# Score matmuls on partition halves, and a new order of scores and attention x V

## The chip, the cores and the metric

The kernel runs on one core of a Trainium2 chip. The metric is the device time of one execution in microseconds (us); the median of several runs counts. The engines are TensorE (PE; its weight loads are listed apart as PEld), VectorE (DVE), ScalarE (ACT), GpSimd (POOL) and SyncE (SP), which here issues every DMA transfer.

## The reference

Sigmoid attention for 2 batches of 12 heads, 448 tokens and head size 64, then an RMS norm, a gated MLP and a SiLU MLP over 896 tokens of 768 features. The MLP weights are float64.

```python
scores = scale * np.matmul(q, k.transpose(0, 1, 3, 2)) - np.log(S)
attn = 1.0 / (1.0 + np.exp(-scores))
attn_out = np.matmul(attn, v)                       # per batch and head
x = attn_out.transpose(0, 2, 1, 3).reshape(B * S, H * D)
xn = x / np.sqrt(np.mean(x * x, -1, keepdims=True) + 1e-6) * rms_g
g = xn @ w_gate
x = (g * sigmoid(g) * (xn @ w_val)) @ w_out         # 768 -> 1536 -> 768
h = x @ w_in                                        # 768 -> 2048
out = (h * sigmoid(h)) @ w_out2                     # 2048 -> 768
```

## The kernel before, in words

Everything is kept feature-major: features on the 128 partitions, tokens along the free dimension. A float32 operand is split into two float32r parts, a high part (a rounded copy) and a low part (the value minus the copy), and a product is made of several matmuls of such parts. Attention x V is a plain float32 matmul, which shows in the trace as two TensorE records per matmul.

**Attention** goes over 12 pairs of heads, a pair being two heads of one batch. For pair i, `load_pair` (lines 157 to 162) brings keys and queries from arrays in which the host has stored every head twice, once on each half of the partitions: a tile is [128, 2 heads, 448]. `prep` (lines 168 to 179) makes the parts. `ks` holds the high part of the keys on partitions 0 to 63 and the low part on 64 to 127; `qs` holds the high part of the queries on both halves, and beside it the low part on both halves. So one matmul over 128 rows computes (high + low keys) x high queries, a second one the same with low queries: two per head in `scores` (lines 181 to 194), for one chunk of 112 keys and all 448 queries. A pair has four chunks. A tile of keys or queries is 448 KB; for pair 0 each head's half, 224 KB, is loaded by itself. One ScalarE instruction then reads both heads' scores from PSUM and writes the sigmoids (line 193). `attend` multiplies a chunk with V, the two heads into the two halves of the output partitions, accumulating over the four chunks (line 202). `collect` copies two pairs' outputs from PSUM; `square` and `add_squares` gather the squares for the RMS norm.

The order is written by hand (`manual_schedule`): every engine runs its instructions in the order in which the program lists them. In pair i's turn the program lists the split of pair i+1, the loads of pair i+2, and then per chunk c: scores of (i, c), attention x V of (i-1, c), and one step of a generator. For pairs 1 to 7 that generator converts the first four weight slabs (float64 words to float32r parts, ScalarE and VectorE); from pair 8 on it is the first batch's norm: square sums by matmul (line 242), reciprocal root on VectorE (lines 249 to 259), its spread over the partitions by a matmul (line 269), and the scaling.

All PSUM is one pool of four tiles of two banks, [128, 2, 512] floats. A chunk's scores take one tile, a head to each bank; an attention x V result takes one for two pairs.

**The MLPs** follow from line 360 on, every product through `product` (line 106), with weight slabs loaded and converted ahead. The first two gate units' first batch is computed ahead of them while the second batch is normed.

Of the kernel before, what the change touches and what calls it, by code (L numbers as in the profile page):

```python
# [8 lines left out]
F32 = mybir.dt.float32  # L9
# [11 lines left out]
P = 128  # L21
# [10 lines left out]
def tile_attention_two_mlps(  # L32
    ctx: ExitStack,
    tc: tile.TileContext,
    qd: bass.AP,
    kd: bass.AP,
    vd: bass.AP,
# [4 lines left out]
):  # L42
    """sigmoid attention -> RMS norm -> gated MLP -> SiLU MLP, feature-major throughout.

    Every float32 product is hi*hi + lo*hi + hi*lo of float32r halves (12 + 12 bits), except
    attention x V, which is a plain float32 matmul. The float64 weights are narrowed to float32 on chip:
    P = the high word read as float32; P * 2^-112 moves the 11-bit exponent to float32's bias, the
    shift by 3 lines it up, and the sign and the low word's top 3 bits are put in.
    """
    nc = tc.nc  # L50
# [10 lines left out]

# [1 line left out]
    nslab = wd.shape[0]  # L63
# [7 lines left out]
    def convert(s):  # L71
        """Yields between steps, so that no engine's queue waits behind another's step."""
        words = raw_t.pop(s).rearrange("p (n two) -> p n two", two=2)
        low, high = words[:, :, 0], words[:, :, 1]
        f = wtmp.tile([P, SLAB], F32, tag="f", name=f"f{s}")
        fu = f.bitcast(U32)
        nc.scalar.activation(f, high.bitcast(F32), AF.Copy, scale=2.0**-112)  # L77
        yield
        nc.vector.tensor_scalar(fu, fu, 3, None, ALU.logical_shift_left)  # L79
        nc.vector.scalar_tensor_tensor(fu, high, 0x80000000, fu, ALU.bitwise_and, ALU.bitwise_or)  # L80
        nc.vector.scalar_tensor_tensor(fu, low, 29, fu, ALU.logical_shift_right, ALU.bitwise_or)  # L81
        yield
        yield
        t = wsp.tile([P, 2, SLAB], F32R, tag="w", name=f"w{s}")
        nc.scalar.activation(t[:, 0, :], f, AF.Copy)  # L85
        yield
        nc.vector.tensor_tensor(t[:, 1, :], f, t[:, 0, :].bitcast(F32), ALU.subtract)  # L87
        slab_t[s] = t
# [5 lines left out]
    def split(dst, src):  # L94
        """dst[:, 0] + dst[:, 1] = src, in float32r halves."""
        nc.scalar.activation(dst[:, 0], src, AF.Copy)  # L96
        nc.vector.tensor_tensor(dst[:, 1], src, dst[:, 0].bitcast(F32), ALU.subtract)  # L97

    def product(ps, tiles, acts, bs, last=True):
        """ps[:, b, :S] += W^T x for the weight tiles and activations given, over b in bs."""  # L100
        n = len(tiles)
        for i, (w, a) in enumerate(zip(tiles, acts)):
            whi, wlo = wtile(w)
            for lhs, j in ((whi, 0), (whi, 1), (wlo, 0)):
                for b in bs:
                    nc.tensor.matmul(  # L106
                        ps[:, b, :S],
                        lhs,
                        a[:, j, b * S : (b + 1) * S],
                        start=(i == 0 and j == 0 and lhs is whi),  # L110
                        stop=(i == n - 1 and lhs is wlo),
                    )
            if last and w % 6 == 5:
                del slab_t[w // 6]
                ahead(w // 6 + 1 + AHEAD)
# [15 lines left out]
    def ahead(s):  # L131
        """Slabs before s converted, and the loads two slabs on."""
        fetch(s + 2)
        while sched[0] < min(s, nslab):
            for _ in convert(sched[0]):
                pass
            sched[0] += 1
# [7 lines left out]

# [1 line left out]
    ctx.enter_context(tc.manual_schedule())  # L147
    with ExitStack() as actx:
        ap = actx.enter_context(tc.tile_pool(name="ap", bufs=2))
        at = actx.enter_context(tc.tile_pool(name="at", bufs=6))  # L150
        npool = actx.enter_context(tc.tile_pool(name="npool", bufs=1))

        pairs = [(b, hp) for b in range(B) for hp in range(NP)]
        qr, kr, vr, qs, ks, att, av, xraw, acc = {}, {}, {}, {}, {}, {}, {}, {}, {}

        def load_pair(i):
            b, hp = pairs[i]
            kr[i] = ap.tile([P, 2, S], F32, tag="kr", name=f"kr{i}")
            qr[i] = ap.tile([P, 2, S], F32, tag="qr", name=f"qr{i}")
            for hs in (slice(0, 1), slice(1, 2)) if i == 0 else (slice(0, 2),):  # L160
                nc.sync.dma_start(kr[i][:, hs], kd[b, hp, :, hs])  # L161
                nc.sync.dma_start(qr[i][:, hs], qd[b, hp, :, hs])  # L162

# [4 lines left out]
        def prep(i):  # L168
            k, q = kr.pop(i), qr.pop(i)
            ks[i] = kst = ap.tile([P, 2, S], F32R, tag="ks", name=f"ks{i}")  # L170
            qs[i] = qst = ap.tile([P, 2, 2, S], F32R, tag="qs", name=f"qs{i}")
            for hs in (slice(0, 1), slice(1, 2)) if i == 0 else (slice(0, 2),):
                nc.vector.tensor_copy(kst[:, hs], k[:, hs])
                if i:
                    nc.vector.tensor_copy(qst[:, 0, hs], q[:, hs])
                else:
                    nc.scalar.activation(qst[:, 0, hs], q[:, hs], AF.Copy)  # L177
                nc.vector.tensor_tensor(kst[D:, hs], k[D:, hs], kst[D:, hs].bitcast(F32), ALU.subtract)  # L178
                nc.vector.tensor_tensor(qst[:, 1, hs], q[:, hs], qst[:, 0, hs].bitcast(F32), ALU.subtract)  # L179

        def scores(i, c):
            ps = ps_tile(f"sc{i}_{c}")
            for h in range(2):
                for j in range(2):
                    nc.tensor.matmul(  # L185
                        ps[:CP, h, :S],
                        ks[i][:, h, c * CP : (c + 1) * CP],
                        qs[i][:, j, h, :],
                        start=(j == 0),
                        stop=(j == 1),  # L190
                    )
            a = at.tile([CP, 2, S], F32, tag="a", name=f"a{i}_{c}")
            nc.scalar.activation(a, ps[:CP, :, :S], AF.Sigmoid, bias=logs[:CP], scale=D**-0.5)  # L193
            att[i, c] = a
# [15 lines left out]
        def collect(i):  # L210
            """Two pairs' outputs from PSUM, and their squares."""
            b, hp = pairs[i]
            if hp % 2 == 0:
                return
            ps = av.pop(i // 2)
            t = npool.tile([P, 2, S], F32, tag=f"xr{b}_{hp // 2}", name=f"xr{b}_{hp // 2}")
            nc.vector.tensor_copy(t, ps[:, :, :S])
            xraw[b, hp // 2] = t
            fresh.append((b, hp))
# [19 lines left out]
        def square_sums(b, ps):  # L239
            """ps[t, c] = the sum of squares of token c * 112 + t."""  # L240
            for c in range(NC):
# [4 lines left out]
        def rsqrt(b, ps):  # L246
            """diag[t, c, u] = eye[t, u] / rms of token c * 112 + t; Newton steps from the exponent's half."""
            ms, y, t = (npool.tile([CP, NC], F32, tag=n, name=f"{n}{b}") for n in ("ms", "y", "t"))
# [18 lines left out]
        def spread(ps, diag):  # L267
            """ps[:, t] = 1 / rms of token t, on every partition."""
            nc.tensor.matmul(ps, ones[:CP], diag.rearrange("p c u -> p (c u)"), start=True, stop=True)  # L269

        def normed(b, r):
            """Yields between steps, like convert."""
            xn, xs = {}, {}
# [40 lines left out]
        for i in range(n):  # L314
# [5 lines left out]
            if i == 0:  # L320
                fetch(1)
            for c in range(NC):
                scores(i, c)
                if c == 1:
                    square()
                if c == 3:
                    add_squares()
                if i:
                    attend(i - 1, c)
                if 0 < i <= NP + 1 and c:  # L330
                    next(weights, None)
                if i > NP + 1:
                    next(normal, None)
            if i:
# [6 lines left out]

        # the first two gate units' first batch, while the second batch is normed
        for _ in itertools.chain(weights, normal):
# [15 lines left out]

# [1 line left out]
    hp_ = ctx.enter_context(tc.tile_pool(name="hp", bufs=1))  # L361
# [44 lines left out]
def _slabs(w, nk):  # L406
    """[K, M] float64 as 64-bit words: 128 x 128 tiles, output chunk by output chunk, six to a slab."""
    import numpy as np
# [42 lines left out]
```

## Time and profile before

| | us |
|---|---|
| median of 3 runs | 605.83 (604.96 to 1182.08) |
| span of the profiled execution | 604.1 |
| busy in it: TensorE, its weight loads | 592.8, 503.4 |
| busy in it: VectorE, ScalarE | 354.1, 230.1 |

The page names the profiled execution's span, from its first to its last instruction; the median run is 1.7 us above it (605.83 - 604.1), and no further time of that execution is listed. The mean granted TensorE clock is 0.999. Busy times of engines overlap. TensorE's two rows are the matmuls and the weight loads that run beside them.

### The profile page before, as it was taken

The page shows a single profiled execution, that of the slowest core. Times are in us where ns is not written, and L with a number is a line of the kernel's source. Part 1 is how long each engine was busy: PE and PEld are TensorE (multiplying, and loading weights), DVE is VectorE, ACT ScalarE, POOL GpSimd, SP SyncE. Part 2 cuts the span into 40 slices and gives each one's busy share as a digit, 9 for nine tenths or more (in the row PEclk, how much of TensorE's full clock was granted, in tenths as well). Part 3 has the DMA queues.
Part 4 walks back from the last instruction along what each step waited for, and adds up shares of the span by engine and source line. Part 5 has one row for each costly group of instructions (what it writes and reads, how often), then busy time and mean ns, then how long its engine had stood idle before and what let it go on. Part 6 is the DMA issues. An engine that isn't in the chain of part 4 may idle for free.

```text
span 604.1 us, 6969 instructions
## 1 busy us (share of the span) xinstructions
PE 592.8 (98%) x2852; PEld 503.4 (83%) x2852; DVE 354.1 (59%) x444; ACT 230.1 (38%) x271; POOL 0.2 (0%) x4
## 2 busy tenths in 40 slices
PE   4999999999999999999999999999999999999997
PEld 3444445999999999999999999999999999999996
DVE  4788793767766666666555554666666555545500
ACT  4676574344433333333333223444444432222100
POOL 0000000000000000000000000000000000000000
PEclk9999999999999999999999999999999999999999
DMA  8655540024333333232433333233332343433000
GB/s 248 225 204 206 204 144 0 1 105 150 132 137 105 105 105 105 104 105 104 129 123 115 105 105 105 105 105 105 104 105 104 106 143 120 134 135 136 30 31 30
DMA packets 16383, 70.49 MB, mean 117 GB/s; under 512 B 2080, under 2 KB 2848, under 8 KB 16352
## 3 DMA queue, kind: packets, MB, share of 16 engines
q1 hardware_dynamic: 16352, 70.05, 34.0%
q8 instruction: 22, 0.36, 0.3%
q14 instruction: 9, 0.07, 0.0%
HBM read 67.29 MB, written 2.75 MB: 116 GB/s over the span
## 4 chain that ended last, share of the span: by engine, by line
PE 97%; DMA 1%; DVE 1%; SPq 0%; issue 0%
PE e L106 19%; PE i L106 19%; PE g L106 15%; PE v L106 15%; PE o L106 14%; PE sc L185 7%; PE av L202 7%; DMA qr<-in_q 1%; SPq L161 0%; DVE ks L178 0%; DVE qs L179 0%; PE r L269 0%; PE ms L242 0%; SPq L162 0%; PE v L269 0%; PE v L242 0%
## 5 line engine op out<-in xcount | busy, mean ns | idle before, releaser
L85 ACT ACTIVATE w<-f 128x768 fp32r<-128x768 f32 x68 | 57.5, 846 | 277.8 <-PE i L106 62.7
L87 DVE TENSOR_TENSOR w<-f,w 128x768 fp32r<-128x768 f32 x68 | 65.2, 958 | 150.4 <-ACT w L85 150.4
L106 PE MATMUL e<-g,w 128*128 128x448 f32 x576 | 116.9, 365 | 0.0
L106 PE MATMUL i<-y,w 128*128 128x448 f32 x576 | 116.9, 365 | 0.0
L106 PEld LDWEIGHTS i<-y,w 128*128 128x128 f32 x576 | 108.2, 188 | 8.5
L106 PEld LDWEIGHTS e<-g,w 128*128 128x128 f32 x576 | 108.2, 188 | 8.5
L106 PE MATMUL g<-x,w 128*128 128x448 f32 x432 | 90.3, 366 | 0.0
L106 PE MATMUL v<-x,w 128*128 128x448 f32 x432 | 89.9, 365 | 0.0
L106 PE MATMUL o<-h,w 128*128 128x448 f32 x432 | 87.7, 365 | 0.0
L106 PEld LDWEIGHTS g<-x,w 128*128 128x128 f32 x432 | 81.1, 188 | 7.5 <-issue 0.9
L106 PEld LDWEIGHTS o<-h,w 128*128 128x128 f32 x432 | 81.2, 188 | 6.4
L106 PEld LDWEIGHTS v<-x,w 128*128 128x128 f32 x432 | 81.1, 188 | 6.4
L185 PEld LDWEIGHTS sc<-qs,ks 128*112 128x112 f32 x192 | 31.5, 182 | 42.0 <-issue 24.9
L80 DVE SCALAR_TENSOR_TENSOR f<-raw,f 128x768 uint32<-128x768 uint32 x68 | 65.2, 958 | 2.3
L81 DVE SCALAR_TENSOR_TENSOR f<-raw,f 128x768 uint32<-128x768 uint32 x68 | 65.2, 958 | 2.4
L185 PE MATMUL sc<-qs,ks 128*112 128x448 f32 x192 | 53.9, 404 | 7.7 <-ACT qs L177 7.2
L77 ACT ACTIVATE f<-raw 128x768 f32<-128x768 f32 x68 | 60.8, 894 | 1.1 <-DMA raw<-in_w 1.1
L193 ACT ACTIVATE a<-sc,logs 112x896 f32<-112x896 f32 x48 | 48.2, 1007 | 27.6 <-PE sc L185 27.0
L202 PE MATMUL av<-a,vr 112*64 112x448 f32 x192 | 45.8, 562 | 0.0
L79 DVE TENSOR_SCALAR f<-f 128x768 uint32<-128x768 uint32 x68 | 37.6, 553 | 4.5 <-ACT f L77 4.5
L401 DVE COPY out<-e 128x896 f32<-128x896 f32 (+1 forms) x7 | 6.7, 957 | 32.3 <-PE e L106 32.3
L97 DVE TENSOR_TENSOR g<-sg,g 128x896 fp32r<-128x896 f32 x16 | 17.5, 1093 | 13.3 <-ACT g L96 13.3
(49 smaller groups left out, 198.1 us busy)
## 6 DMA issues: line engine op xcount, KB each, us to landing
raw<-in_w SPq DMA_DIRECT2D x68, 768.0 KB, 4.2
kr<-in_k SPq DMA_DIRECT2D x11, 448.0 KB, 5.0
qr<-in_q SPq DMA_DIRECT2D x11, 448.0 KB, 5.6
vr<-in_v SPq DMA_DIRECT2D x12, 224.0 KB, 2.8
out_t<-out SPq DMA_DIRECT2D x5, 448.0 KB, 2.5
kr<-in_k SPq DMA_DIRECT2D x2, 224.0 KB, 3.3
qr<-in_q SPq DMA_DIRECT2D x2, 224.0 KB, 4.2
out_t<-out SPq DMA_DIRECT2D x2, 224.0 KB, 1.9
```

Source lines behind the costliest of these rows:

```text
L77: nc.scalar.activation(f, high.bitcast(F32), AF.Copy, scale=2.0**-112)
L79: nc.vector.tensor_scalar(fu, fu, 3, None, ALU.logical_shift_left)
L80: nc.vector.scalar_tensor_tensor(fu, high, 0x80000000, fu, ALU.bitwise_and, ALU.bitwise_or)
L81: nc.vector.scalar_tensor_tensor(fu, low, 29, fu, ALU.logical_shift_right, ALU.bitwise_or)
L85: nc.scalar.activation(t[:, 0, :], f, AF.Copy)
L87: nc.vector.tensor_tensor(t[:, 1, :], f, t[:, 0, :].bitcast(F32), ALU.subtract)
L97: nc.vector.tensor_tensor(dst[:, 1], src, dst[:, 0].bitcast(F32), ALU.subtract)
L106: nc.tensor.matmul(ps[:, b, :S], lhs, a[:, j, b * S : (b + 1) * S], start=(i == 0 and j == 0 and lhs is whi), stop=(i == n - 1 and lhs is ...
L185: nc.tensor.matmul(ps[:CP, h, :S], ks[i][:, h, c * CP : (c + 1) * CP], qs[i][:, j, h, :], start=(j == 0), stop=(j == 1),)
L193: nc.scalar.activation(a, ps[:CP, :, :S], AF.Sigmoid, bias=logs[:CP], scale=D**-0.5)
L202: nc.tensor.matmul(ps[h * D : (h + 1) * D, hp % 2, :S], vr[i][:, c, h, :], a[:, h, :], start=(c == 0), stop=(c == NC - 1),)
L401: nc.vector.tensor_copy(o[:, sl], ps[:, sl, :S])
```

## The change

Keys and queries are no longer stored twice. The host lays a pair's two heads on the two halves of the partitions, keys and queries side by side in one array, and one tile `kq` (three buffers) holds both. `prep` makes the high part of the whole tile and the low part of the whole tile. `scores` runs three matmuls per head on 64 rows each, high x high, high keys x low queries, low keys x high queries, the two heads in turns; the product of the two low parts is not computed any more. In the loop over chunks, two chunks' scores are followed by attention x V of two chunks, and the generators' steps stand behind them, three and four per pair as before. The sigmoid tiles have eight buffers instead of six.

```diff
-        at = actx.enter_context(tc.tile_pool(name="at", bufs=6))
+        at = actx.enter_context(tc.tile_pool(name="at", bufs=8))
...
-            kr[i] = ap.tile([P, 2, S], F32, tag="kr", name=f"kr{i}")
-            qr[i] = ap.tile([P, 2, S], F32, tag="qr", name=f"qr{i}")
-            for hs in (slice(0, 1), slice(1, 2)) if i == 0 else (slice(0, 2),):
-                nc.sync.dma_start(kr[i][:, hs], kd[b, hp, :, hs])
-                nc.sync.dma_start(qr[i][:, hs], qd[b, hp, :, hs])
+            kq[i] = ap.tile([P, 2, S], F32, tag="kq", name=f"kq{i}", bufs=3)
+            if i:
+                nc.sync.dma_start(kq[i], qkd[b, hp])
+            else:
+                for j in range(2):
+                    nc.sync.dma_start(kq[i][:, j], qkd[b, hp, :, j])
...
-            ks[i] = kst = ap.tile([P, 2, S], F32R, tag="ks", name=f"ks{i}")
-            qs[i] = qst = ap.tile([P, 2, 2, S], F32R, tag="qs", name=f"qs{i}")
-            for hs in (slice(0, 1), slice(1, 2)) if i == 0 else (slice(0, 2),):
-                nc.vector.tensor_copy(kst[:, hs], k[:, hs])
-                if i:
-                    nc.vector.tensor_copy(qst[:, 0, hs], q[:, hs])
-                else:
-                    nc.scalar.activation(qst[:, 0, hs], q[:, hs], AF.Copy)
-                nc.vector.tensor_tensor(kst[D:, hs], k[D:, hs], kst[D:, hs].bitcast(F32), ALU.subtract)
-                nc.vector.tensor_tensor(qst[:, 1, hs], q[:, hs], qst[:, 0, hs].bitcast(F32), ALU.subtract)
+            raw = kq.pop(i)
+            ks[i] = kst = ap.tile([P, 2, 2, S], F32R, tag="ks", name=f"ks{i}")
+            if i:
+                nc.vector.tensor_copy(kst[:, 0], raw)
+                nc.vector.tensor_tensor(kst[:, 1], raw, kst[:, 0].bitcast(F32), ALU.subtract)
+            else:
+                nc.vector.tensor_copy(kst[:, 0, 0], raw[:, 0])
+                nc.scalar.activation(kst[:, 0, 1], raw[:, 1], AF.Copy)
+                for j in (1, 0):
+                    nc.vector.tensor_tensor(
+                        kst[:, 1, j], raw[:, j], kst[:, 0, j].bitcast(F32), ALU.subtract
+                    )
...
-            for h in range(2):
-                for j in range(2):
+            for step, (jk, jq) in enumerate(((0, 0), (0, 1), (1, 0))):
+                for h in range(2):
+                    rows = slice(h * D, (h + 1) * D)
                     nc.tensor.matmul(
                         ps[:CP, h, :S],
-                        ks[i][:, h, c * CP : (c + 1) * CP],
-                        qs[i][:, j, h, :],
-                        start=(j == 0),
-                        stop=(j == 1),
+                        ks[i][rows, jk, 0, c * CP : (c + 1) * CP],
+                        ks[i][rows, jq, 1, :],
+                        start=(step == 0),
+                        stop=(step == 2),
                     )
...
-            for c in range(NC):
+            for c in range(0, NC, 2):
                 scores(i, c)
-                if c == 1:
+                scores(i, c + 1)
+                if c == 0:
                     square()
-                if c == 3:
+                else:
                     add_squares()
                 if i:
                     attend(i - 1, c)
-                if 0 < i <= NP + 1 and c:
-                    next(weights, None)
-                if i > NP + 1:
-                    next(normal, None)
+                    attend(i - 1, c + 1)
+                for _ in range(1 if c == 0 else 2):
+                    if 0 < i <= NP + 1:
+                        next(weights, None)
+                for _ in range(2):
+                    if i > NP + 1:
+                        next(normal, None)
...
     def headwise(a):
-        t = a.transpose(0, 1, 3, 2).reshape(B, NP, 2, D, S).transpose(0, 1, 3, 2, 4)
-        return np.ascontiguousarray(np.concatenate([t, t], axis=2))
+        return a.transpose(0, 1, 3, 2).reshape(B, NP, P, S)
...
-        "q": headwise(q),
-        "k": headwise(k),
+        "kq": np.ascontiguousarray(np.stack([headwise(k), headwise(q)], axis=3)),
```

## Rows read from the trace of the kernel before

**Rows 1.** The page's chain that ended last: share of the span by line.
```profile
PE e L106 19%; PE i L106 19%; PE g L106 15%; PE v L106 15%; PE o L106 14%; PE sc L185 7%; PE av L202 7%; DMA qr<-in_q 1%; SPq L161 0%; DVE ks L178 0%; DVE qs L179 0%; PE r L269 0%; PE ms L242 0%; SPq L162 0%; PE v L269 0%; PE v L242 0%
```

**Rows 2.** Stretches: length; busy us (count) PE, PEld, DVE, ACT, POOL; clock; DMA share; GB/s.
```profile
0.00:14.44 14.44, 6.77 (x17) 4.38 (x17) 6.97 (x13) 6.17 (x8) 0.20 (x4) 1.00 0.88 246
14.44:67.49 53.05, 53.05 (x224) 22.70 (x224) 42.25 (x52) 36.75 (x40) 0.00 (x0) 1.00 0.61 221
```

**Rows 3.** Timeline of TensorE, two chunks: start us, us, line, out<-in, count.
```profile
40.86 1.06 PE L185 MATMUL sc<-qs,ks 128*112 128x448 f32 x4
...
41.85 0.97 PE L202 MATMUL av<-a,vr 112*64 112x448 f32 x4
...
42.76 1.08 PE L185 MATMUL sc<-qs,ks 128*112 128x448 f32 x4
...
44.67 0.46 PE L185 MATMUL sc<-qs,ks 128*112 128x448 f32 x1
```

**Rows 4.** Timeline inside the first of those chunks, from narrow windows.
```profile
41.15 0.57 PE L185 MATMUL sc<-qs,ks 128*112 128x448 f32 x2
...
41.16 0.17 PEld L185 LDWEIGHTS sc<-qs,ks 128*112 128x112 f32 x1
...
41.56 0.37 PE L185 MATMUL sc<-qs,ks 128*112 128x448 f32 x1
...
42.28 0.55 PE L202 MATMUL av<-a,vr 112*64 112x448 f32 x2
```

**Rows 5.** Chain in order of time, one MLP product: start us, us, what.
```profile
148.15 7.30 PE g L106 x36
```

**Rows 6.** Timeline after the last scores: five chunks of attention x V.
```profile
98.56 3.98 PE L202 MATMUL av<-a,vr 112*64 112x448 f32 x20
...
98.99 0.14 PEld L202 LDWEIGHTS av<-a,vr 112*64 112x64 f32 x2 [0.23 <-issue]
...
101.62 0.14 PEld L202 LDWEIGHTS av<-a,vr 112*64 112x64 f32 x2 [0.23 <-issue]
...
102.47 0.88 PE L106 MATMUL g<-x,w 128*128 128x448 f32 x3
```

**Rows 7.** Groups by line and shape, 0 to 150 us: busy us, mean ns, idle before.
```profile
L193 ACT ACTIVATE a<-sc,logs 112x896 f32<-112x896 f32 x48 | 48.2, 1007 | 27.6 <-PE sc L185 27.0
...
L179 DVE TENSOR_TENSOR qs<-qr,qs 128x896 fp32r<-128x896 f32 x11 | 12.0, 1092 | 0.3
...
L77 ACT ACTIVATE f<-raw 128x768 f32<-128x768 f32 x10 | 8.9, 891 | 1.1 <-DMA raw<-in_w 1.1
...
L175 DVE CAST qs<-qr 128x896 fp32r<-128x896 f32 x11 | 6.8, 621 | 1.7 <-DMA qr<-in_q 1.7
...
L225 ACT ACTIVATE sq<-xr 128x896 f32<-128x896 f32 x6 | 5.7, 944 | 4.0 <-DVE xr L217 4.0
```

**Rows 8.** Timeline of the start, 0 to 20 us.
```profile
4.51 0.63 DVE L179 TENSOR_TENSOR qs<-qr,qs 128x448 fp32r<-128x448 f32 x1
...
4.56 1.35 PE L185 MATMUL sc<-qs,ks 128*112 128x448 f32 x2 [4.56 <-ACT qs L177]
...
7.91 0.58 ACT L177 ACTIVATE qs<-qr 128x448 fp32r<-128x448 f32 x1 [3.42 <-DMA qr<-in_q]
...
8.53 5.42 PE L185 MATMUL sc<-qs,ks 128*112 128x448 f32 x15 [2.62 <-ACT qs L177]
...
9.75 0.63 DVE L173 CAST ks<-kr 128x896 fp32r<-128x896 f32 x1 [0.61 <-DMA kr<-in_k]
...
13.30 1.09 DVE L179 TENSOR_TENSOR qs<-qr,qs 128x896 fp32r<-128x896 f32 x1
...
14.44 0.86 PE L185 MATMUL sc<-qs,ks 128*112 128x448 f32 x3 [0.49 <-DVE qs L179]
```

**Rows 9.** Timeline of the first batch's norm on VectorE: first step, diagonal.
```profile
70.94 0.15 DVE L249 TENSOR_SCALAR ms<-ms 112x4 f32<-112x4 f32 x1
...
73.31 0.62 DVE L259 TENSOR_TENSOR diag<-eye,y 112x448 f32<-112x448 f32 x1
```

More of the change, by code (lines that the diff above doesn't have):

```diff
@@ L34, in tile_attention_two_mlps @@
     tc: tile.TileContext,
-    qd: bass.AP,
-    kd: bass.AP,
+    qkd: bass.AP,
     vd: bass.AP,
@@ L149, in tile_attention_two_mlps @@
         ap = actx.enter_context(tc.tile_pool(name="ap", bufs=2))
-        at = actx.enter_context(tc.tile_pool(name="at", bufs=6))
+        at = actx.enter_context(tc.tile_pool(name="at", bufs=8))
         npool = actx.enter_context(tc.tile_pool(name="npool", bufs=1))
         pairs = [(b, hp) for b in range(B) for hp in range(NP)]
-        qr, kr, vr, qs, ks, att, av, xraw, acc = {}, {}, {}, {}, {}, {}, {}, {}, {}
+        kq, vr, ks, att, av, xraw, acc = {}, {}, {}, {}, {}, {}, {}
         def load_pair(i):
             b, hp = pairs[i]
-            kr[i] = ap.tile([P, 2, S], F32, tag="kr", name=f"kr{i}")
-            qr[i] = ap.tile([P, 2, S], F32, tag="qr", name=f"qr{i}")
-            for hs in (slice(0, 1), slice(1, 2)) if i == 0 else (slice(0, 2),):
-                nc.sync.dma_start(kr[i][:, hs], kd[b, hp, :, hs])
-                nc.sync.dma_start(qr[i][:, hs], qd[b, hp, :, hs])
+            kq[i] = ap.tile([P, 2, S], F32, tag="kq", name=f"kq{i}", bufs=3)
[4 more added lines that the diff above has]
+                    nc.sync.dma_start(kq[i][:, j], qkd[b, hp, :, j])
         def load_v(i):
@@ L168, in prep @@
         def prep(i):
-            k, q = kr.pop(i), qr.pop(i)
-            ks[i] = kst = ap.tile([P, 2, S], F32R, tag="ks", name=f"ks{i}")
-            qs[i] = qst = ap.tile([P, 2, 2, S], F32R, tag="qs", name=f"qs{i}")
-            for hs in (slice(0, 1), slice(1, 2)) if i == 0 else (slice(0, 2),):
-                nc.vector.tensor_copy(kst[:, hs], k[:, hs])
-                if i:
-                    nc.vector.tensor_copy(qst[:, 0, hs], q[:, hs])
-                else:
-                    nc.scalar.activation(qst[:, 0, hs], q[:, hs], AF.Copy)
-                nc.vector.tensor_tensor(kst[D:, hs], k[D:, hs], kst[D:, hs].bitcast(F32), ALU.subtract)
-                nc.vector.tensor_tensor(qst[:, 1, hs], q[:, hs], qst[:, 0, hs].bitcast(F32), ALU.subtract)
+            raw = kq.pop(i)
[10 more added lines that the diff above has]
+                    )
         def scores(i, c):
             ps = ps_tile(f"sc{i}_{c}")
-            for h in range(2):
-                for j in range(2):
+            for step, (jk, jq) in enumerate(((0, 0), (0, 1), (1, 0))):
+                for h in range(2):
+                    rows = slice(h * D, (h + 1) * D)
                     nc.tensor.matmul(
                         ps[:CP, h, :S],
-                        ks[i][:, h, c * CP : (c + 1) * CP],
-                        qs[i][:, j, h, :],
-                        start=(j == 0),
-                        stop=(j == 1),
+                        ks[i][rows, jk, 0, c * CP : (c + 1) * CP],
+                        ks[i][rows, jq, 1, :],
+                        start=(step == 0),
+                        stop=(step == 2),
                     )
```

## Prediction

> **What bounds the kernel now.** I read the chain of waits first, then a table by stretches, then the timeline of a few rounds. The chain is TensorE nearly throughout, 14% of the span on the two lines that the change rewrites [rows 1]. A busy matmul engine in this profile only means that some matmul is in flight, so the question is what each one costs in its place. The stretches [rows 2] show a start to 14.44 us, in which TensorE is busy for 6.8 and otherwise waits, and after it attention with TensorE busy without a gap, VectorE at 80% and ScalarE at 69%. Since TensorE never pauses from 14.44 on, what attention loses or gains moves everything behind it by as much. The MLPs, from 102.47 on [rows 6], are not touched, so the sum is about 0 to 102.5 us alone.
>
> TensorE's timeline in that stage is a strict alternation [rows 3]: a block of four score matmuls, a block of four attention x V records, two chunks in 3.81 us (40.86 to 44.67), 1.90 for a round. The starts inside one round [rows 3, 4] say where that goes. Score matmuls start at 40.86, 41.15 and, two further on, 41.56: a spacing of 0.29, then 0.41 for two, then 0.29 to the first attention x V record at 41.85. Those records come in twos, one per head, which write different halves of the output partitions and are in flight together; the second two start at 42.28, the next scores at 42.76: 0.43 and 0.48. What they cost without neighbours of another shape stands elsewhere: a long run of equal products takes 7.30 us for 36, 0.203 each [rows 5], and where five chunks of attention x V follow one another a new two start every 0.376 us (eight from 98.99 to 101.62, (101.62 - 98.99) / 7) [rows 6]. So four scores should cost 0.81 and two twos 0.75; the remaining 0.33 us (0.09 + 0.09 + 0.05 + 0.10) is paid for changing from one shape to the other and back, once per round.
>
> **The change part by part.**
>
> *The score matmuls.* Removed: 2 matmuls per head and chunk on all 128 rows, four slots of 0.203. Added: 3 per head on 64 rows, the heads on different halves, in turns. No row shows two matmuls on different row halves. [...] From this I take one pair of heads as one slot of p = 0.203, three slots per chunk. [...] I take 0.203 because the row with two in flight is nearer in kind, and because each head has its own weights, inputs and PSUM bank.
>
> *The order.* Two chunks of scores, then two of attention x V: one change of shape and back per two chunks, 0.33 instead of 0.67. What changing between row halves and column halves costs is not shown; bounds 0 and 0.67, taken 0.33, since the attention x V side of the change is the same.
>
> Two chunks then cost 6 x 0.203 + 4 x 0.375 + 0.33 = 3.05 us instead of 3.81, 0.76 less. From pair 1 on there are 11 pairs of two such rounds, 22: **16.7 us**. By parts, 22 x 0.406 = 8.9 from two matmul slots fewer and 22 x 0.33 = 7.3 from the order; the last 0.5 is that two chunks of before read 3.81 and build up to 3.79.
>
> *The loads and the split.* Per pair two transfers of 448 KB become one. On VectorE two casts of 0.62 and two subtractions of 1.09, 3.42 us, become one of each, 1.71 [rows 7]. In the steady stage both lie beside TensorE, which never waits for them, so I count nothing; the cover is one pair's time, which shrinks from 7.6 to 6.1 us. VectorE then has 42.25 / 7 - 1.71 = 4.3 us of work per pair and ScalarE, whose work is unchanged, 36.75 / 7 = 5.25: 86% [rows 2]. The transfers run at 221 GB/s there, 1.68 MB per pair; less 0.46 MB in 6.1 us that is 200, under what is reached now. SP keeps its order: the load of V for two pairs on waits until a V tile is free at the end of a pair, and the next load of keys and queries queues behind it, but that one has a whole pair's time before its split. The generators' steps come in twos behind attention x V instead of singly; they are the same instructions, and the ones that TensorE waits for are in the norm, below.
>
> *The start.* Here the loads are on the path [rows 8]. The first score matmul starts at 4.56, on the first head's keys and queries; TensorE then waits for the second head's (ScalarE gets its queries at 7.91, the fourth transfer of 224 KB), and pair 1's scores for another 896 KB and their split, whose last subtraction begins at 13.30 and releases them at 14.44. Afterwards the first two transfers hold both heads and the third is all of pair 1. The first matmul stays at 4.56; the low part of the queries is ready at 5.14, that of the keys one 0.63 later at 5.8, where chunk 0 issues its last two. [...] Nine more slots take 3.3 and the one before 0.4: pair 0 is through at 9.6. By 7.91 four times 224 KB had landed in the old order; now keys, queries and all of pair 1 are just as much, so pair 1 lands by 7.9, and cast and subtraction add 1.71: 9.6 too. Pair 1 starts 14.44 - 9.6 = **4.8 us** earlier.
>
> *The rest.* The norm of the first batch has VectorE work between two TensorE steps, 3.0 us from 70.94 to the end of the diagonal at 73.93 [rows 9]. Three rounds, 5.7 us, stand between those steps now; one of 3.05 will. The diagonal is then just late, with its semaphores: I charge **0.5 us**. Of the four PSUM tiles attention x V holds one; the second chunk of a block of scores takes the tile of the first of the block before, which its sigmoid has read some 1.75 us after that block began, while it is wanted 3.65 after: nothing.
>
> Sum: 16.7 + 4.8 - 0.5 = 21.0 us off a span of 604.1. The median of the runs, 605.83, lies 1.7 above that span, which I carry over: 605.8 - 21.0 = **584.8 us**.
>
> **The rivals.**
>
> *The halves overlap only in part* (598 us). If a head's next weights can't load while its own half streams, each step pays the 0.29 to 0.30 of a first score matmul: 6 x 0.30 + 1.83 = 3.63, 0.18 less than now, 22 x 0.18 = 4.0; with 4 of the start that is 598. Against it: inside the block of scores a weight load starts at 41.16 together with the matmul before it, on the same rows [rows 4]. [...] Chance 0.09.
>
> *The heads take turns* (615 us or more, slower). If two row halves that write the same 112 PSUM partitions are served one after the other, two chunks have 12 slots: 12 x 0.203 + 1.83 = 4.27, 0.46 more than now, 22 x 0.46 = +10.1; the start gives back only about 0.9, as 24 matmuls at 0.36 fill it: 605.8 + 9.2 = 615. With the fill on each (0.30) it would be some 642. For it: no row shows row halves. It decides from p = 0.366 on, where 6p + 1.83 = 3.81 + 4.8 / 22. Chance 0.07.
>
> *ScalarE sets the pace* (590 us). A round with a square and a conversion holds it for 2 x 1.01 + 0.94 + 0.89 = 3.85 us [rows 7] against 3.05. Six rounds have a square; with none of the PSUM slack, 6 x 0.8 = 4.8 us. For it: the 86%. Against: rounds without a square give the time back. Chance 0.08.
>
> *Pair 1 starts later* (587): if its transfer lands only where pair 1's keys do now (cast at 9.75 [rows 8]), its scores start at 11.5, 1.9 us later. This lies inside my own range.
>
> **How the numbers follow.** Forecast 0.76, partial overlap 0.09, ScalarE 0.08, turns 0.07. The forecast's own range: p from 0.1875 (-2) to 0.24 (+5), the change of shape from half to one and a half times 0.33 (-3.6 to +3.6), the start +-2, not all at once: 580 to 592. Up to 598 come ScalarE and most of the partial overlap; left out are the turns and the extremes, some 0.15 with the edge. A change of 2% is 12.1 us, about what a measurement tells from none: faster than 593.7 are nearly all of the forecast (0.74) and most of the ScalarE case (0.07); within 2% are partial overlap, half of the turns and the remainder (0.15); slower by more is the worse half of the turns (0.04).
>
> **What would show it.** Two score matmuls starting some 10 ns apart, the next two 0.20 later (wrong: one every 0.20); two chunks in 3.05 us; pair 1 at 9.6; the first MLP product at 81.5 instead of 102.47; MLP products still 7.30 per 36. Idle of TensorE before scores, released by a sigmoid, would be the ScalarE case. I am wrong if twos of heads start more than 0.3 us apart.

## The result, and the profile after

The changed kernel takes 585.13 us (median of 4 runs, 584.93 to 586.01) against 605.75 before; the ratio is 0.967, 95% interval 0.966 to 0.969. One run of the kernel before took 1182.08 us, nearly twice as long as the others (604.96 to 605.83), and stays out of the ratio. The forecast was 584.8 us, 580 to 598.

The chain of waits of the kernel after, by line: the score line has gone from 7 to 6% of a shorter span, attention x V stays at 7% [rows 1].

```profile
PE e L106 20%; PE i L106 20%; PE g L106 15%; PE v L106 15%; PE o L106 15%; PE av L206 7%; PE sc L189 6%; DMA kq<-in_kq 0%; PE r L273 0%; PE ms L246 0%; PE v L273 0%; PE v L246 0%; DVE out L409 0%; ACT ks L178 0%; SPq L163 0%
```

The same kernel by stretches (length; busy us PE, PEld, DVE, ACT, POOL; clock; DMA share; GB/s): the start up to pair 1's first scores, and pairs 1 to 7, as in [rows 2].

```profile
0.00:9.13 9.13, 4.51 (x24) 3.33 (x26) 3.53 (x8) 4.47 (x6) 0.20 (x4) 1.00 0.79 229
9.13:51.93 42.80, 42.80 (x283) 20.35 (x279) 31.07 (x38) 36.28 (x41) 0.00 (x0) 1.00 0.58 201
```

The start is 9.13 us long instead of 14.44, and seven pairs take 42.80 us instead of 53.05. That is 14 blocks of two chunks, 3.057 us each. A block of before is 3.804: its stretch begins at pair 1's second score matmul (2 + 15 stand ahead of 14.44 in [rows 8], and pair 0 has 16), so one matmul's 0.2 us belongs to it and not to the start, and (53.05 + 0.2) / 14 = 3.804. TensorE is still busy without a gap, VectorE has fallen to 31.07 / 42.80 = 73%, ScalarE risen to 36.28 / 42.80 = 85%.

TensorE's timeline, one block of two chunks, and narrow windows at the first and last of its scores (start us, us, line, count), which answer to [rows 3] and [rows 4].

```profile
30.48 1.48 PE L189 MATMUL sc<-ks 64*112 64x448 f32 x12
31.89 1.72 PE L206 MATMUL av<-a,vr 112*64 112x448 f32 x8
33.55 0.45 PE L189 MATMUL sc<-ks 64*112 64x448 f32 x2
...
30.48 0.46 PE L189 MATMUL sc<-ks 64*112 64x448 f32 x2
...
31.59 0.38 PE L189 MATMUL sc<-ks 64*112 64x448 f32 x2
```

Two score matmuls start together, at 30.48 and again at 31.59, where the sixth two stands: (31.59 - 30.48 - 0.09) / 5 = 0.204 us for each two, the 0.09 being what a block's first step takes longer (0.29 for 0.20, as in [rows 3, 4]). Such a step from one start to the next is called a slot below. Twelve matmuls of 64 rows take six slots; before, eight matmuls of 128 rows took eight.

The start, and the norm's step between the batches (the same timeline's columns), which answer to [rows 8] and [rows 9]; last, the first MLP product.

```profile
7.18 0.63 DVE L174 CAST ks<-kq 128x896 fp32r<-128x896 f32 x1 [1.42 <-DMA kq<-in_kq]
...
7.84 1.09 DVE L175 TENSOR_TENSOR ks<-kq,ks 128x896 fp32r<-128x896 f32 x1
...
8.94 0.36 PE L189 MATMUL sc<-ks 64*112 64x448 f32 x2
...
10.44 1.72 PE L206 MATMUL av<-a,vr 112*64 112x448 f32 x8
...
58.34 0.63 DVE L263 TENSOR_TENSOR diag<-eye,y 112x448 f32<-112x448 f32 x1
...
59.12 0.99 PE L273 MATMUL r<-diag,ones 112*128 112x448 f32 x2
...
81.44 0.86 PE L106 MATMUL g<-x,w 128*128 128x448 f32 x3
```

Pair 0's last scores start at 8.94 and pair 1's next, 0.20 later. The first MLP product starts at 81.44 instead of 102.47 [rows 6], 21.03 earlier; behind it nothing has changed, 36 products still take 7.30 us (7.30 in [rows 5]).

### The profile page after: what moved, and what is told of

Read it like the earlier page. It is cut to its first block, busy times and chain, and to the rows that moved or that the text cites. A ratio compares the mean times of both kernels' runs of the same rounds, so it can differ in the third digit from the quotient of the medians.

```text
span 583.0 us, 7116 instructions
## 1 busy us (share of the span) xinstructions
PE 574.8 (99%) x2948; PEld 498.5 (85%) x2948; DVE 334.7 (57%) x419; ACT 226.8 (39%) x270; POOL 0.2 (0%) x4
## 4 chain that ended last, share of the span: by engine, by line
PE 99%; DMA 0%; DVE 0%; ACT 0%; SPq 0%; issue 0%
PE e L106 20%; PE i L106 20%; PE g L106 15%; PE v L106 15%; PE o L106 15%; PE av L206 7%; PE sc L189 6%; DMA kq<-in_kq 0%; PE r L273 0%; PE ms L246 0%; PE v L273 0%; PE v L246 0%; DVE out L409 0%; ACT ks L178 0%; SPq L163 0%
## 5 line engine op out<-in xcount | busy, mean ns | idle before, releaser
L197 ACT ACTIVATE a<-sc,logs 112x896 f32<-112x896 f32 x48 | 45.8, 1007 | 11.0 <-PE sc L189 10.7
L189 PEld LDWEIGHTS sc<-ks 64*112 64x112 f32 x288 | 24.8, 179 | 22.2 <-ACT a L197 9.9
L189 PE MATMUL sc<-ks 64*112 64x448 f32 x288 | 37.0, 391 | 4.6 <-ACT ks L178 4.6
L206 PE MATMUL av<-a,vr 112*64 112x448 f32 x192 | 40.9, 551 | 0.0
L206 PEld LDWEIGHTS av<-a,vr 112*64 112x64 f32 x192 | 11.8, 136 | 19.2 <-issue 19.2
```

The source lines that it names most:

```text
L189: nc.tensor.matmul(ps[:CP, h, :S], ks[i][rows, jk, 0, c * CP : (c + 1) * CP], ks[i][rows, jq, 1, :], start=(step == 0), stop=(step == 2),)
L206: nc.tensor.matmul(ps[h * D : (h + 1) * D, hp % 2, :S], vr[i][:, c, h, :], a[:, h, :], start=(c == 0), stop=(c == NC - 1),)
```

## The experiments

Every kernel is compared with runs of the kernel before on the same chip, which took 605.29 to 605.40 us. The changed kernel itself, beside three of the others: 585.66 us, ratio 0.968 (0.966 to 0.969).

> The changed kernel itself, beside the others of this group: 585.1.

**The halves without the order.** The changed kernel with the loop over single chunks of the kernel before:

```diff
-            for c in range(0, NC, 2):
+            for c in range(NC):
                 scores(i, c)
-                scores(i, c + 1)
...
```

> The new scores on partition halves, but one chunk of scores and one of attention x V in turn, as before. Theory (the gain is two matmul slots per two chunks, half of the changes of shape, and the start, about 9, 7 and 5 us): a round is 3 x 0.203 + 2 x 0.375 + 0.33 = 1.69 us, two are 3.39 against 3.07 in the changed kernel, 22 x 0.32 = 7 us more: 592. Rival (the order brings all that is not the start, the halves nothing): 600. Rival (the halves bring all, the order nothing): 585.

592.41 us, ratio 0.979 (0.978 to 0.981). Its timeline, TensorE, one round:

```profile
41.37 0.86 PE L189 MATMUL sc<-ks 64*112 64x448 f32 x6
42.15 0.97 PE L206 MATMUL av<-a,vr 112*64 112x448 f32 x4
43.05 0.86 PE L189 MATMUL sc<-ks 64*112 64x448 f32 x6
```

43.05 - 41.37 = 1.68, as built from the parts (1.69). Without the new order 6.8 us (592.41 - 585.66) of the 20 are missing; the rest is there.

**The order without the halves.** The kernel before with the changed kernel's loop and eight sigmoid buffers.

```diff
-            for c in range(NC):
+            for c in range(0, NC, 2):
                 scores(i, c)
+                scores(i, c + 1)
...
                     attend(i - 1, c)
+                    attend(i - 1, c + 1)
...
```

> The kernel before (two matmuls per head on all rows, keys and queries stored twice) with the new order of two chunks each and eight sigmoid buffers. Theory: two chunks cost 8 x 0.203 + 4 x 0.375 + 0.33 = 3.46 us instead of 3.81, 22 x 0.35 = 7.7 us less, start as before: 598. Rival (the order brings nothing): 605.8. With the run above the parts should add up: 605.8 - 7.7 - 9 - 5 = 584.

597.27 us, ratio 0.987 (0.985 to 0.988): 8.1 us less than before. Its timeline:

```profile
40.97 1.89 PE L185 MATMUL sc<-qs,ks 128*112 128x448 f32 x8
42.79 1.72 PE L202 MATMUL av<-a,vr 112*64 112x448 f32 x8
44.45 1.87 PE L185 MATMUL sc<-qs,ks 128*112 128x448 f32 x8
```

Two chunks in 3.48 us instead of 3.81, 22 x 0.33 = 7.3 us. The other 0.8 lies in the start of this run and is not the order's: the second head's queries came sooner, so that the scores went on at 7.36 us instead of 8.53 [rows 8]. The parts add up: 7.3 from the order, and 605.34 - 592.41 = 12.9 from the halves with the start above, 20.2 together against the 19.6 to 20.6 measured for the whole.

**The same rows for both heads.**

```diff
-                    rows = slice(h * D, (h + 1) * D)
+                    rows = slice(0, D)
```

> The changed kernel with both heads' matmuls on partitions 0 to 63: the second head's scores are computed from the first head's keys and queries, so the output is not the reference's; instructions and sizes are the same. Theory (it is the different halves that let two run at a time): twelve slots per two chunks, 12 x 0.203 + 1.83 = 4.27 us against 3.07, 22 x 1.2 = 26.4 us more, and some 3 more in the start where 24 matmuls stand in place of 12 pairs: 614. Rival (two 64-row matmuls are cheap by themselves, whichever half): 585.

623.07 us, ratio 1.028 (1.025 to 1.031), slower than the kernel before. Timeline of one block:

```profile
42.27 2.69 PE L189 MATMUL sc<-ks 64*112 64x448 f32 x12
44.90 1.72 PE L206 MATMUL av<-a,vr 112*64 112x448 f32 x8
46.55 0.66 PE L189 MATMUL sc<-ks 64*112 64x448 f32 x2
```

46.55 - 42.27 = 4.28: on one half the twelve matmuls are twelve slots, a hundredth from what the rival of heads that take turns was priced at (4.27). So it is the different halves that make the pairs. The 9 us beyond 614 lie in the first 34 us, where the slots stayed long: the block that starts at 18.23 in the changed kernel starts at 33.73 here. Some pieces of the same kernel's chain in order of time (start us, us, what):

```profile
21.46 4.75 PE sc L189 x12
...
29.40 2.75 PE sc L189 x12
...
33.80 2.62 PE sc L189 x12
```

A block of scores takes 4.75 us at 21.46 and 2.62 at 33.80, the change falling into the one at 29.40. TensorE had been at work without a gap since 4.50; in the changed kernel pair 0's twos start at 7.81, 8.19, 8.53, 8.73 and 8.94, so that the slots shrink at about 8.5 us. The granted clock reads 1.00 over both lengths of slot (4.50 to 29.60 and 29.60 to 40.00 in this run), so the change is read from the slots alone, from 0.38 us (7.81 to 8.19) to 0.20 (8.53 to 8.73) in the changed kernel; its cause is not shown.

**One head after the other.**

```diff
-            for step, (jk, jq) in enumerate(((0, 0), (0, 1), (1, 0))):
-                for h in range(2):
+            for h in range(2):
+                for step, (jk, jq) in enumerate(((0, 0), (0, 1), (1, 0))):
```

> The changed kernel with a head's three matmuls in a row, then the other head's three, instead of in turns. Theory (matmuls start in the order of the program, two are in flight only where neighbours lie on different halves): of twelve matmuls in two chunks three neighbours overlap, nine slots instead of six, 22 x 3 x 0.203 = 13.4 us more, and about 1.5 more in the start: 600. Rival (TensorE runs the halves side by side in whatever order they are queued): 585.

586.41 us, ratio 0.969 (0.968 to 0.970). The theory fell. TensorE's timeline: the first matmuls of the start, from narrow windows, then a steady block and the two starts in front of it.

```profile
4.55 1.37 PE L189 MATMUL sc<-ks 64*112 64x448 f32 x2 [4.55 <-ACT ks L178]
...
5.21 1.25 PE L189 MATMUL sc<-ks 64*112 64x448 f32 x3
...
31.83 0.46 PE L189 MATMUL sc<-ks 64*112 64x448 f32 x2
...
31.83 1.49 PE L189 MATMUL sc<-ks 64*112 64x448 f32 x12
33.26 1.72 PE L206 MATMUL av<-a,vr 112*64 112x448 f32 x8
34.91 1.27 PE L189 MATMUL sc<-ks 64*112 64x448 f32 x10
```

In the steady block the first two matmuls start together at 31.83. On one half there was only one at a time (the run above, 4.28 us for a block), so the second is the other head's first, which the program lists as the fourth: it passed two matmuls of the first head. The block of two chunks is 3.08 us (34.91 - 31.83), as in turns. In the start, where the first head's matmuls wait for low parts, they start alone (4.55, then 5.21) and the other head's only beside the third (three in flight at 5.75), though the high parts that it needs were there for both heads (in turns both start at 4.62). So a matmul that waits did hold back the other half's behind it. The 0.8 to 1.3 us more than in turns lie there: attention x V first starts at 11.76 instead of 10.44. About 0.4 of that is two more slots; the rest is that the slots shrank at about 10.5 us in this execution instead of 8.5.

**Six of a head in a row.** Both chunks' matmuls of the first head, then those of the second:

```diff
-        def scores(i, c):
+        def scores(i, cs):
...
+            for h in range(2):
+                rows = slice(h * D, (h + 1) * D)
+                for c, ps in zip(cs, pss):
+                    for step, (jk, jq) in enumerate(((0, 0), (0, 1), (1, 0))):
...
```

> The changed kernel with the first head's six matmuls of two chunks in a row, then the second head's six. With three in a row the halves still ran side by side, so matmuls do not start in program order across halves. Theory (each half works through its own queue as far as TensorE has fetched ahead, at least twelve matmuls): still six slots per two chunks in the steady rounds, 3.07 us; the start, where the second head now waits behind the first head's low parts, up to 1.5 more; and the first chunk's sigmoid starts 0.6 us later: 586 to 588. Rival (it looks only a few matmuls ahead): up to 11 slots, 22 x 5 x 0.203 = 22 us more: 608.

596.45 us, ratio 0.986 (0.984 to 0.987), between the two. TensorE's timeline, narrow windows first:

```profile
30.69 0.45 PE L190 MATMUL sc<-ks 64*112 64x448 f32 x1
...
30.99 0.56 PE L190 MATMUL sc<-ks 64*112 64x448 f32 x2
...
31.19 0.66 PE L190 MATMUL sc<-ks 64*112 64x448 f32 x4
...
30.69 1.97 PE L190 MATMUL sc<-ks 64*112 64x448 f32 x12
32.60 1.72 PE L208 MATMUL av<-a,vr 112*64 112x448 f32 x8
34.25 1.99 PE L190 MATMUL sc<-ks 64*112 64x448 f32 x12
```

Two start alone (30.69, 30.99); from the third on, at 31.19, both halves work. From there the other head's six take what six slots take elsewhere: 32.60 - 31.19 = 1.41 us up to attention x V, as 31.89 - 30.48 in the changed kernel. So a block is longer by the 0.50 us that the other head starts late: 34.25 - 30.69 = 3.56 us, 22 x 0.50 = 11.0 more, and 10.8 were measured (596.45 - 585.66). Neither expectation had this. The other head's first is the seventh in the program here and starts beside the third, when the fourth, which waits for the second chunk's PSUM tile, comes up. Whether TensorE looks no further than some matmuls ahead, or that wait holds the rest back, as waits did in the start of the run before, isn't told apart.

**More bytes in front of pair 1.**

```diff
         load_pair(0)
+        for j in range(2):
+            junk = ap.tile([P, 2, S], F32, tag="junk", name=f"junk{j}")
+            nc.sync.dma_start(junk, qkd[pairs[2 + j]])
         load_pair(1)
```

> The changed kernel with two more transfers of 448 KB (into a tile that nothing reads) between pair 0's and pair 1's keys and queries, so that as many bytes stand before pair 1's end as in the kernel before. Theory (pair 1's transfer is on the path of the start): its cast starts at about 11.5 instead of 7.2 us, its scores at 13.2 instead of 9.1, 4 us more: 589, and TensorE idle before them. Rival (the start gained because pair 0 has 12 slots instead of 16, loads are covered): 585.

589.40 us, ratio 0.975 (0.972 to 0.977), 3.7 more than the changed kernel beside it. Timeline:

```profile
10.72 0.63 DVE L174 CAST ks<-kq 128x896 fp32r<-128x896 f32 x1 [5.08 <-DMA kq<-in_kq]
...
11.38 1.09 DVE L175 TENSOR_TENSOR ks<-kq,ks 128x896 fp32r<-128x896 f32 x1
...
11.49 0.46 PE L189 MATMUL sc<-ks 64*112 64x448 f32 x2 [1.72 <-DVE ks L174]
...
12.53 1.33 PE L189 MATMUL sc<-ks 64*112 64x448 f32 x10 [0.58 <-DVE ks L175]
```

TensorE waits 1.72 us for the cast and 0.58 for the subtraction. So with as many bytes in front as before, the load of pair 1 is on the path of the start, and pair 0's fewer slots alone would not have brought pair 1 forward. The wait is not all of the difference: the first attention x V behind it takes 16.97 - 13.79 = 3.18 us instead of 1.66, at a granted clock of 0.50 (see the last section).

**VectorE's split twice.**

```diff
                 nc.vector.tensor_tensor(kst[:, 1], raw, kst[:, 0].bitcast(F32), ALU.subtract)
+                more = ap.tile([P, 2, 2, S], F32R, tag="more", name=f"more{i}", bufs=1)
+                nc.vector.tensor_copy(more[:, 0], raw)
+                nc.vector.tensor_tensor(more[:, 1], raw, more[:, 0].bitcast(F32), ALU.subtract)
```

> The changed kernel with the split of every pair from 1 on done twice, the second time into a tile that nothing reads: VectorE has one cast and one subtraction more per pair, 1.71 us, as before the change. Theory (VectorE's saving is hidden in the steady rounds, its place in the start is 1.7 us of slack at most): +1.7 us for pair 1's split or less, nothing later: 585 to 587. Rival (TensorE needs the freed VectorE time in the pairs that also norm, where VectorE would have 8.6 us of work in 6.1): 590 or more, with TensorE idle between 55 and 77 us.

588.74 us, ratio 0.973 (0.971 to 0.975), 3.1 more: the theory fell, and the rival's wait is there at less than its price. TensorE's waits in the first 90 us (who waited for whom: us, times, longest):

```profile
PE r L276 <- DVE diag L266: 1.6, 1, 1.6
PE sc L192 <- DVE xr L224: 1.4, 2, 1.0
```

1.6 us at the norm's spread, waiting for the diagonal, and 1.4 for copies of attention x V results that hold a PSUM tile. In the changed kernel neither wait is listed. So the 1.71 us per pair that the change takes off VectorE are needed: with that work still there, the shorter rounds would have cost 3.1 us.

**Blocks of four chunks**, to see whether fewer changes of shape bring more:

```diff
-            for c in range(0, NC, 2):
+            for c in range(NC):
                 scores(i, c)
-                scores(i, c + 1)
-                if c == 0:
-                    square()
+            square()
+            for c in range(0, NC, 2):
...
```

> The changed kernel with all four chunks of scores before four of attention x V, and one norm step moved a pair later. Theory (a change of shape and back costs 0.33 us): 11 fewer, 3.7 us less, minus a wait of some 0.2 us per pair, because the fourth chunk needs the first one's PSUM tile while its sigmoid has just ended: 583.5. Rival (the PSUM tiles bind, ScalarE's conversions delay the first sigmoid by most of 1 us): 590.

587.34 us, ratio 0.970 (0.969 to 0.972), 1.7 more than blocks of two, between the theory and the rival. One of TensorE's waits (us, times, longest):

```profile
PE sc L189 <- DVE xr L221: 3.1, 4, 1.1
```

and the timeline around its longest:

```profile
34.20 0.96 DVE L81 SCALAR_TENSOR_TENSOR f<-raw,f 128x768 uint32<-128x768 uint32 x1
35.07 1.08 DVE L221 COPY xr<-av 128x896 f32<-128x896 f32 x1
...
36.21 0.86 PE L189 MATMUL sc<-ks 64*112 64x448 f32 x6 [1.04 <-DVE xr L221]
```

The PSUM tiles bind, as the rival says, but not through a sigmoid: the tile is held by an attention x V result, whose copy (35.07) stands on VectorE behind a conversion step (34.20).

**The copy sooner.** In that kernel the copy goes ahead of the conversion steps:

```diff
                     attend(i - 1, c + 1)
+                    if c:
+                        collect(i - 1)
...
-            if i:
-                collect(i - 1)
```

> The run with four chunks in a block, where TensorE waited 3.1 us for the copy of the attention x V result that stood on VectorE behind three conversion steps; here the copy stands ahead of them. Theory (the copy held the PSUM tile, and the 3.7 us of fewer changes of shape come out once it doesn't): 587.3 - 3.1 = 584.2, up to 1 less. Rival (VectorE's backlog only moves to the next wait): 587.

585.11 us, ratio 0.967 (0.966 to 0.968): 2.2 us less than without, 0.9 more than the theory, not to be told apart from the changed kernel. What TensorE still waits for, mostly sigmoids now:

```profile
PE av L206 <- ACT a L197: 0.7, 1, 0.7
PE sc L189 <- ACT a L197: 0.5, 2, 0.3
PE sc L189 <- DVE xr L221: 0.4, 1, 0.4
```

Where nothing waits, the fewer changes of shape do come out. A pair from the timeline:

```profile
21.81 2.70 PE L189 MATMUL sc<-ks 64*112 64x448 f32 x24
...
27.60 2.08 PE L189 MATMUL sc<-ks 64*112 64x448 f32 x18
```

27.60 - 21.81 = 5.79 us for the pair against 42.80 / 7 = 6.11, 0.32 less for one change of shape and back. From pair 8 on, where the norm is, the kernel loses 1.0 us again: 30.47 us up to the first MLP product (51.37 to 81.84) against 29.51 in the changed kernel (51.93 to 81.44).

**Early matmuls**, on top of that:

```diff
+        ps = ps_tile("early")
+        for _ in range(8):
+            nc.tensor.matmul(ps[:, 0, :P], ones, ones, start=True, stop=True)
```

> The same with eight matmuls of a constant tile, 128 columns each, before the first keys have landed, so that TensorE is busy from about 1.1 us on; their result is read by nothing. Theory (the clock rises sooner, pair 0's slots shrink from 0.37 to 0.20 us, then pair 1's split at 8.9 us is the bound): 0.5 to 1 us less than without: 583.4. Rival (the clock does not rise sooner, or the start is bound by the loads alone): no difference.

584.51 us, ratio 0.966 (0.964 to 0.967): the fastest median, 0.6 below the run without, as expected, but the intervals overlap, so it is not shown to beat the changed kernel. Its trace shows the shorter slots sooner; that the clock rose sooner is not shown, since it reads 1.00 from 0 to 5.30 us and from 5.40 to 9.00. Pair 0's twos start 0.20 us apart from 6.03 on, and pair 1 then waits for its subtraction:

```profile
9.18 2.50 PE L189 MATMUL sc<-ks 64*112 64x448 f32 x22 [0.58 <-DVE ks L175]
```

These are pair 1's second two and what follows; in the changed kernel its second two start at 9.34.

**Six sigmoid buffers.**

```diff
-        at = actx.enter_context(tc.tile_pool(name="at", bufs=8))
+        at = actx.enter_context(tc.tile_pool(name="at", bufs=6))
```

> The changed kernel with six sigmoid buffers instead of eight, as before the change. Theory (a sigmoid tile is wanted again only after the attention x V that reads it, which stands ahead of the next two chunks of scores): 585.5. Rival (the two extra tiles carry the order of two chunks): TensorE or ScalarE waits for a tile in each round, 0.3 us or more, 592.

585.38 us, ratio 0.967 (0.966 to 0.969): no difference from the changed kernel (585.13 and 585.66). The two extra tiles carry nothing.

## Why the prediction was right, step by step

*The score matmuls.* Right in mechanism and size: a pair of heads takes one slot, 0.204 us for 0.203 forecast, and the run on one half shows what hangs on the halves (4.28 instead of 3.06 us per block). The 0.203 is the spacing of equal products [rows 5]; that two in flight cost no more than one was carried over from attention x V, whose twos, on column halves, start every 0.376 us [rows 6], while the norm's float32 matmul of 448 columns takes 0.75 us for its two records one after the other (from 89.89 in the changed kernel's chain), 0.375 each. It carried over to row halves without loss. The 0.1875 that the range of p goes down to is half of such a record, an estimate; no run shows a slot that short, the score matmuls' took 0.204. The partial overlap is refuted: the twos stand 0.204 apart though each head loads its next weights on its own rows. Two such loads start at 30.57, while both matmuls that started at 30.48 are in flight (to 30.94), as the load at 41.16 does beside the matmul before it [rows 4].

*The order.* Right: 3.06 - 6 x 0.204 - 4 x 0.375 = 0.34 us per change and back, for row halves as for full rows (0.33). The order alone brought 7.3 of the 8.1 us of its run (forecast 7.3 to 7.7), its absence cost 6.8 to 7.3 (592.41 against 585.66 and 585.13).

*Two chunks.* 3.05 forecast, 3.057 measured (42.80 / 14): 22 x (3.804 - 3.057) = 16.4 us, 16.7 forecast.

*The start.* Right in what bounds it, 0.3 us too small: 14.44 - 0.2 - 9.13 = 5.1 for 4.8, with the 0.2 that belongs to pair 1's first matmul. I carried the spacing of 0.36 (15 in 5.42 us [rows 8]) through all of pair 0, 3.3 us for nine slots; in the run the slots shrink to 0.20 at about 8.5 us. This moment differs between executions: in the run with six sigmoid buffers it comes at about 10 us, and pair 1 starts at 9.60, as forecast. The load was bounded rightly (cast at 7.18, forecast by 7.9). The subtraction ends at 8.93, and pair 1's second two, the first that need it, start at 9.34; in the run with early matmuls, where they wait for it, they start at 9.18. So both bounds nearly meet, as the working said. The run with more bytes in front shows the load on the path.

*The split on VectorE.* Counted at nothing, and TensorE waits for nothing of it. The working named the cover as one pair's time and left it there; at the new pace the doubled split costs 3.1 us. The zero was right for the change as made, but not for the reason given: at the new pace that work would not be covered any more; it is gone.

*The norm.* Charged 0.5 us for a diagonal just late. It ends at 58.97 and the spread starts at 59.12, 0.66 us behind the last two of attention x V (58.46) where 0.48 is usual (54.51 to 54.99): 0.18 late. The two steps together cost 0.4 us more than before: the blocks that hold them take 55.86 - 51.93 = 3.93 and 60.04 - 55.86 = 4.18 us, 0.87 and 1.12 over 3.06; before, the round with the sums took 0.80 over 1.90 (67.49 to 70.19) and the two rounds around the spread 0.77 over 3.80 (73.97 to 78.54). The other 0.24 lies between the steps and the scores behind them, which stand on row halves now and, like the steps, stood on all rows before; that this is the cause is not shown. The term was right in size, its cause mostly another.

*The rivals.* ScalarE did not set the pace at 85%; blocks of four chunks show where it and the PSUM tiles begin to.

Sum against result: 5.1 + 16.4 - 0.4 = 21.1, and the trace of after has 21.0 at the first MLP product, as forecast. That the total came out to a tenth is luck in part: the blocks were put 0.3 us too high and the start 0.3 too low, and the start's share moves with the moment at which the slots shrink.

## What to carry to other kernels

Price a matmul in its place: the difference between a run of equal ones and the same ones between others is the cost of changing shape, here 0.33 us per change and back. Grouping equal shapes two by two halved it (two chunks in 3.48 us instead of 3.81, 0.33 less); with four by four, PSUM tiles were held by somebody else (3.1 us of waits). Contractions over half the rows paid here with another one on the other half: 3.06 us for a block with the heads in turns and 3.08 with three of a head in a row, but 3.56 with six in a row and 4.28 with all on one half. When the bounding engine's round gets shorter, ask of every engine beside it whether its work still fits, and count what the change takes off it towards that.

## What the runs showed of the hardware that was not expected

With three of a head in a row, matmuls on different row halves did not start in the order of the program, though ahead of the prediction every engine is said to run its instructions in the order listed: a head's first matmul passed two of the other head's (starts together at 31.83), and the block was as long as in turns (3.08 us for 3.06). With the other head's first in seventh place it started 0.50 us late (31.19 for 30.69).

With all score matmuls on one half, TensorE's slots stayed long (4.75 us for twelve, 2.62 later) until the block at 29.40 us, although it had worked without a gap from 4.50; attention x V was long with them (3.25 us at 26.14, 1.72 at 32.07). With both halves in use they shrank at about 8.5 us in the changed kernel, and between 8.6 and 10.8 in the other runs (8.9 in its second, 10.8 with the copy sooner), earlier only behind the early matmuls (0.20 apart from 6.03 on). What sets the moment is not shown. In the run with more bytes in front, the granted clock of the stretch from 13.60 to 17.00 us was 0.50, after TensorE had waited 1.72 and 0.58 us; that the waits are the cause is not shown (columns as in the stretches above):

```profile
13.60:17.00 3.40, 3.40 (x12) 0.79 (x10) 1.72 (x2) 1.54 (x2) 0.00 (x0) 0.50 0.88 302
17.00:20.00 3.00, 3.00 (x22) 1.43 (x20) 1.81 (x3) 2.70 (x3) 0.00 (x0) 1.00 0.04 14
```
